# A new late half of a hand-written issue order in a fused S5 scan and Hedgehog attention kernel

## Chip, cores and metric

The kernel runs on one core of one Trainium2 chip. Its time is the device time in microseconds (us) of one execution; where several executions are shown, the median counts. Lower is better. Engines are named as the profile names them: PE (TensorE), PEld (its weight loads), DVE (VectorE), ACT (ScalarE), POOL (GpSimd) and SP (SyncE, which here only issues DMAs).

## What is computed

Two sequence mixers run on the same 2048 x 512 input, and a gate mixes them row by row. Branch `a` is a diagonal complex state space model: a projection, a linear recurrence over 2048 steps, a projection back and a skip term. Branch `b` is linear attention with 32 heads of 16 channels, whose feature map is two softmaxes.

```python
g = sigmoid((x * gate_w).sum(-1, keepdims=True))
# a: state space model
Bu = einsum("bld,pd->blp", x + 0j, B_bar)
for t in range(L):
    h = Lam_bar[None, :] * h + Bu[:, t, :]
a = 2.0 * einsum("blp,dp->bld", hseq, Cmat).real + x * Dskip
# b: linear attention, phi(u) = [softmax(u), softmax(-u)] of 16 channels through w_phi
kv = einsum("bhsf,bhsd->bhfd", phi_k, v)
z = einsum("bhsf->bhf", phi_k)
num = einsum("bhqf,bhfd->bhqd", phi_q, kv)
den = einsum("bhqf,bhf->bhq", phi_q, z)[..., None] + 1e-6
b = reshape(num / den) @ wo
return g * a + (1 - g) * b
```

## The kernel before

The 2048 rows are 16 tiles of 128 rows, regrouped so that a tile holds every eighth row; `order[n]` says which tile is the n-th in the late part. The recurrence is cut into eight residues of the row number: a scan over 256 steps is done for residue 7 (`st_z`), and the other residues follow from it by small diagonal products (`st_h`, PE product `ph`, lines 657 to 676).

The work is written as some 270 small generators, each of which issues a few instructions and yields. One string, `ORDER`, lists their names; the loop at lines 817 to 827 takes a name at a time and lets that generator go on to its next yield. PE, DVE, ACT and SP then keep exactly the order in which the list issued their instructions; each engine runs its own queue in order and waits on semaphores where an operand comes from another engine or from a DMA. So the list is a schedule by hand. A name can carry `@` and digits, the PSUM banks (of eight) that its products take, and `:D` or `:A`. `:D` lets DVE instead of ACT copy or scale a PSUM tile; `:A` lets ACT instead of SP issue an output DMA.

The late half of the list is made of these:

- `q4` to `q15`: queries of tile n, four PE products of 512 columns (line 476), copied into `Xq`.
- `h..`: states of one residue, two or four PE products of 256 columns.
- `X1` to `X3`, `N1` to `N3`, `E1` to `E3`, `S1` to `S3`: the feature map of the queries in groups of four tiles. `X` and `N` are DVE maximum and minimum trees and a subtraction, `E` is four ACT exponentials of 1024 columns (line 534, recorded at line 139), `S` is a DVE sum tree, ACT logarithm and exponential, a DVE product, and four DMA transposes on SP that make `phT` (line 564). Group 3 feeds tiles 12 to 15.
- `y0` to `y15`: branch `a` of tile n in a PSUM bank `py`: eight products of 512 columns (line 718), then four of 128 columns (line 723).
- `o0` to `o15`: branch `b` before the output projection. For each of two halves, four PE products of 68 columns give `pn` (line 737); then ACT takes the logarithm of the denominators (`ld`, line 740) and ACT or DVE copies the numerators (`nu`, line 741). ACT makes `rd` (line 743), DVE multiplies (`on`, line 745), and the result is transposed into `oT`: for n below 12 by a DMA on SP (line 759), for 12 to 15 by four PE transposes into a bank `po` and a copy (lines 751 to 757).
- `t0` to `t15`: four products of 512 columns with `Wo` added to `py` (line 766), the gate scaling to `ot` (lines 775 to 780), and the output DMA (lines 782 to 786). For n = 14 (`LAST`) the scaling and the DMA go in two halves, one on ACT, the other on DVE.

Two resources tie these together. A PSUM bank can be written again only when the engines that read its last contents are done; where ACT's `ld` and DVE's `nu` read the same `pn`, DVE waits for ACT, and PE for DVE. And each DMA has one of eight semaphores (named DMAHW0 to DMAHW7 in the order rows); a DMA waits, on the engine that issues it, until the last DMA on the same semaphore has landed.

Of the kernel before, what the change touches and what calls it, by code (L numbers as in the profile page):

```python
# [36 lines left out]
R6 g23@3 v12@2 c4 c0 c0 g63@5 nA z2 z2 a3 a3 g03@4 xA g03 z2 z2 z2 z2 xA g23 z2 z2 g33@6 c5 v12 z2 z2 g13@0 g13 g63  # L37
g43@4 h32@3 g13 nA g43 h52@2 h52 g33 h32 h61@5 h61 h12@0 c0 g53@4 h12 g33 g53 s4 v14@3 c2 eA eA h42@2 h42 g73@6 g53 eA
eA g73 g73 q10@5 sA h11@0 h11 O h00@4 g73 sA v13@2 h00 v13 a4 z3 sA v15@6 z3 v15 h20@0 h01@4 h30@2 v14 h20 sA h30 z3
h31@6 z3 z3 sA a4 h01 h31 c6 c6 sA q13@3 q13 z3 a4 a4 Y Y h22@0 G q10 z3 z3 G q6@2 q6 h22 z3 z3 sA sA Y Y c1 c1 q9@4  # L40
q8@6 q5@7 h62@3 h41@5 c3 h41 c1 c3 c3 h13@0 h62 q11@2 h13 q11 q8 q12@1 c6 q12 h21@5 q5 h21 h02@2 c7 q4@6 q4 h53@3 h53
h23@1 h23 h33@0 h33 sA q9 h40@7 h40 sA q7@5 h43@6 h63@3 c7 h43 q7 c7 y4@0 y4 sA h63 sA h03@1 END h02 o0@4 o0 X1 N1
o1@7 o1 q14@6 X1 N1 h03 o0@5 X1 o1@2 o1 o1 o0 o0 q15@3 o2@4 o2 o2@7 o2 N1 q15 X1 N1 X1 N1 E1 E1 y2@1 y1@2 y1 E1 E1 q14
X2 y0@5 y0 o1 y4 X2 N2 X2 o0 o0 o3@4 o3 o3@7 o3 o1 o3 y2 X2 N2 o2 X2 N2 S1 S1 N2 S1 o3 S1 N2 S1 S1 o3 y5@3 o2 o2 S1 S1
S1 y1 E2 E2 E2 E2 y9@6 G N3 y5 y5 y3@4 y2 X3 X3 N3 t1 G t1 N3 S1 N3 S2 y9 y9 S2 S2 S1 S1 S2 y3 y3 t3 y0 t0 t0 t2 t2
y6@7 X3 t2:A o4@2 o4 o4@5 o4 o4 y6 y6 t3 X3 o4 X3 o4 S2 S2 t3 o5@1 o5 o5@2 o5 o5 y13@5 y13 o5 N3 o6@4 S2 o6 o6@1 o6 o6
y12@2 o5 y7@4 y7 y12 o6 o6 t4 y7 S2 S2 t4:D S2 E3 E3 E3 E3 S2 o7@1 o7 t5 t5 S3 o7@0 o7 S3 o7 t6 S3 o7 S2 o7 y8@1 o8@3
t6 o8 o8@0 o8 o8 S3 S3 y12 t0:A y11@7 o8 o8 o9@3 o9:D o9@0 o9:D S3 y8 y8 o9 o9 S3 S3 o9 o10@3 y11 o10 o10@0 y11 o10
o10 S3 y14@3 S3 y14 t7 t7:D t8 y14 t8 y15@0 o11@4 S3 o11 o11@1 t9 o12@4 o11:D o11 S3 o10 o10 o12 o12@1 o12 o12 t9:D
o11 y15 o13@4 o13:D o13@6 t6:A o13 o13 o11 o12 y10@1 o14@4 y15 o14:D o12@6 t9 o12:D t7:A t1 y10 y10 o13 o15@4 o15  # L50
o15@6 t4:A t5 o15 o15 t8 o15 t12 t12 t12:A t10 o14@4 o14 o14 t10:D o13@6 t11 o15@2 o15 t10 o13:D t11 t11:A y13 t13 o14
o14@1 t15 t13 t13 t15 t15 o14:D t14 t14 t14:A
"""
H_VECTOR = tuple((r, j) for r in (1, 2, 4, 5, 6) for j in range(4))
OT_PE = (12, 13, 14, 15)
# [805 lines left out]
```

## Time and profile before

| | us |
|---|---|
| median of 3 executions | 157.1 (155.83 to 157.33) |
| profiled execution, its own time | 155.2 |
| span of its instructions | 153.1 |
| PE busy | 147.5 (96%) |
| DVE busy | 133.1 (87%) |
| ACT busy | 129.3 (84%) |
| POOL busy | 15.8 (10%), nothing after the first quarter |

The span runs from the first to the last instruction of the program; the profiled execution's own time has 2.1 us around it. In a view of instructions a row is: start, duration, engine, line, operation, tiles written and read, and in square brackets the idle time of that engine before it with what ended it. `SPq` and `ACTq` are DMA issues. In grouped views the number behind `x` counts instructions and the last ones are busy time and mean duration in ns. "to landing" is the time from the issue of a DMA to its completion.

### The profile page before, as it was taken

How to read it: one execution, taken by the hardware profiler on the slowest of the kernel's cores; microseconds unless marked ns; L12 is line 12 of the kernel's file. 1: busy time of each engine (PE TensorE's matmuls, PEld its weight loads, DVE VectorE, ACT ScalarE, POOL GpSimd, SP SyncE). 2: the span in 40 equal slices, each digit the busy share in tenths (PEclk: the TensorE clock that was granted, in tenths of full speed). 3: DMA queues.
4: the chain of work that ended last, by engine and by line, in shares of the span. 5: the costliest groups of instructions: out<-in, count | busy, mean ns of one | idle time of the engine just before them, and what ended most of it. 6: DMA issues, size and time to landing. Idle time of an engine off the chain costs nothing.

```text
span 153.1 us, 3382 instructions
## 1 busy us (share of the span) xinstructions
PE 147.5 (96%) x1254; PEld 95.5 (62%) x1254; DVE 133.1 (87%) x304; ACT 129.3 (84%) x279; POOL 15.8 (10%) x43
## 2 busy tenths in 40 slices
PE   7999979999999999999999999999999999999990
PEld 7844434788878986869867656555555555546550
DVE  3799999999999999999999999999999858716441
ACT  3589998999998999999998999699488998618471
POOL 8239980000000000000000000000000000000000
PEclk9999999999999999999999999999999999999999
DMA  4785996494455699720000007911159959989943
GB/s 122 158 215 77 232 160 143 99 79 104 103 107 100 133 222 178 167 97 4 0 0 4 0 0 167 76 37 33 36 98 144 178 125 187 168 139 186 255 145 104
DMA packets 50992, 17.55 MB, mean 115 GB/s; under 512 B 44192, under 2 KB 50976, under 8 KB 50976
## 3 DMA queue, kind: packets, MB, share of 16 engines
q1 hardware_dynamic: 49120, 15.82, 57.0%
q10 hardware_dynamic: 1696, 1.51, 3.1%
q8 instruction: 10, 0.16, 0.5%
q0 software_dynamic: 160, 0.01, 0.2%
q14 instruction: 6, 0.05, 0.2%
HBM read 2.64 MB, written 2.10 MB: 31 GB/s over the span
## 4 chain that ended last, share of the span: by engine, by line
PE 80%; SPq 9%; DMA 8%; issue 1%; DVE 0%; ACT 0%
PE pgq L602 18%; PE py L718 16%; PE py L766 9%; PE pq L476 9%; SPq L230 7%; DMA xT<-in_A_x_dram 5%; PE pk L476 5%; PE pv L476 5%; PE ph L669 4%; DMA phT<-EEq 3%; PE kvacc L579 3%; PE pn L737 3%; PE pgq L607 2%; PE py L723 2%; PE pgq L609 2%; SPq L285 1%
## 5 line engine op out<-in xcount | busy, mean ns | idle before, releaser
L602 PE MATMUL pgq<-xT,BT 128*128 128x256 bf16 x256 | 31.5, 273 | 0.0
L476 PEld LDWEIGHTS <-xT 128*128 128x128 bf16 x192 | 18.1, 97 | 19.2 <-DMA xT<-in_A_x_dram 1.7
L602 PEld LDWEIGHTS <-BT 128*128 128x128 bf16 x256 | 24.6, 98 | 4.1
L139 ACT ACTIVATE EEk<-EEk 128x1024 bf16<-128x1024 bf16 x20 | 20.5, 1082 | 0.0
L120 ACT CAST uv<-pgq 128x512 bf16<-128x512 f32 x28 | 15.9, 605 | 0.7 <-PE pgq L602 0.5
L766 PE MATMUL py<-Wo,oT 128*128 128x512 bf16 x64 | 15.9, 380 | 0.0
L476 PE MATMUL pv<-Wv,xT 128*128 128x512 bf16 x64 | 15.8, 379 | 0.0
L476 PE MATMUL pq<-Wq,xT 128*128 128x512 bf16 x64 | 15.6, 379 | 0.0
L476 PE MATMUL pk<-Wk,xT 128*128 128x512 bf16 x64 | 14.8, 380 | 0.8 <-DMA xT<-in_A_x_dram 0.8
L139 ACT ACTIVATE EEq<-EEq 128x1024 bf16<-128x1024 bf16 x12 | 11.7, 1043 | 0.2 <-DVE EEq L528 0.2
L139 ACT ACTIVATE ld<-pn 128x16 f32<-128x16 f32 x32 | 6.1, 191 | 6.1 <-PE pn L737 4.7
L778 ACT ACTIVATE ot<-py,G 128x512 bf16<-128x512 f32 x11 | 7.4, 689 | 4.0 <-PE py L766 3.6
L591 ACT ACTIVATE phT<-X,dgB 128x512 bf16<-128x512 bf16 x16 | 10.7, 725 | 0.0
L120 ACT CAST nu<-pn 128x256 bf16<-128x256 f32 x27 | 9.9, 381 | 0.0
L745 DVE TENSOR_TENSOR on<-nu,rd 128x512 bf16<-128x512 bf16 x16 | 6.7, 421 | 3.5 <-ACT rd L139 1.8
L120 ACT CAST Xq<-pk 128x512 bf16<-128x512 f32 x15 | 8.6, 597 | 1.3 <-PE pk L476 1.3
L120 ACT CAST vx<-pv 128x512 bf16<-128x512 f32 x16 | 9.1, 603 | 0.4 <-PE pv L476 0.4
L549 DVE TENSOR_TENSOR EEk<-EEk,rck 128x4096 bf16<-128x4096 bf16 (+1 forms) x5 | 9.3, 1859 | 0.0
L120 ACT CAST Xq<-pq 128x512 bf16<-128x512 f32 x16 | 8.9, 609 | 0.2 <-PE pq L476 0.2
L766 PEld LDWEIGHTS <-oT 128*128 128x128 bf16 x64 | 5.5, 97 | 5.7 <-DMA oT<-on 0.8
L737 PEld LDWEIGHTS <-phT 128*128 128x128 bf16 x128 | 6.3, 97 | 3.5 <-DMA phT<-EEq 0.8
L512 DVE TENSOR_TENSOR smk<-smk 128x512 bf16<-128x512 bf16 (+4 forms) x18 | 8.1, 447 | 0.1
(180 smaller groups left out, 323.9 us busy)
## 6 DMA issues: line engine op xcount, KB each, us to landing
X<-HM SPq DMA_DIRECT2D x8, 256.0 KB, 4.4
out_dram<-ot SPq DMA_DIRECT2D x8, 128.0 KB, 2.2
out_dram<-ot ACTq DMA_DIRECT2D x7, 128.0 KB, 2.7
C2r<-in_B_wqkv_dram ACTq DMA_DIRECT2D x2, 256.0 KB, 3.5
Wv<-in_B_wqkv_dram SPq DMA_DIRECT2D x1, 512.0 KB, 4.1
Bn<-in_A_B_re_dram SPq DMA_DIRECT2D x1, 512.0 KB, 6.4
Bn<-in_A_B_im_dram SPq DMA_DIRECT2D x1, 512.0 KB, 7.2
Wo<-in_B_wo_dram SPq DMA_DIRECT2D x1, 512.0 KB, 4.1
```

What stands on the lines that cost most here:

```text
L120: nc.scalar.copy(out=out_ap, in_=in_ap)
L139: ins = nc.scalar.activation(**kw)
L230: nc.sync.dma_start_transpose(out=xT[:, :, ti * P:(ti + 1) * P], in_=x_res[ti // 2, ti % 2])
L476: MM(out=pt[:], lhsT=xT[:, kt, ti * P:(ti + 1) * P], rhs=W[:, kt, :], start=(kt == 0), stop=(kt == KT - 1))
L512: VT(out=dst, in0=cur[:, :, :, 0:n, :], in1=cur[:, :, :, n:2 * n, :], op=op)
L549: VT(out=E5, in0=E5, in1=rc.to_broadcast([P, L, 2 * NB, Dh, 4]), op=ALU.mult)
L591: nc.scalar.mul(out=t_, in_=x_, mul=c_)
L602: MM(out=pg[:, h, :], lhsT=BT[:, kt, 2 * j + h, :], rhs=xT[:, kt, r * NC:(r + 1) * NC], start=(h == 0 and kt == 0), stop=(r % 2 == 0 and k ...
L718: MM(out=py[:], lhsT=hs(r, t, slice(a * P, (a + 1) * P)), rhs=C2B[t], start=(t == 0), stop=False)
L737: MM(out=pn[:, 4 * m:4 * m + 4, :].rearrange("p h e -> p (h e)"), lhsT=ph[:, 4 * hf + m, :], rhs=KVm[:, 4 * hf + m, :], start=(m == 0), st ...
L766: MM(out=py[:], lhsT=oT[:, g, :], rhs=Wo[:, g, :], start=False, stop=(g == HG - 1))
L778: nc.scalar.mul(out=ot[:], in_=py[:], mul=G[:, ti:ti + 1])
```

## The change

Only the string `ORDER` changes, from the middle of line 40 on: of its 855 names the first 499 stay, and the other 356 are put in another order. The same generators run the same number of times. Other things that the names carry change with it: most PSUM banks, and `:D` or `:A` on some steps, so that three numerator copies and three gate scalings that ACT did are now done by DVE. Two lines of the diff, from the end of the list:

```diff
-o15@6 t4:A t5 o15 o15 t8 o15 t12 t12 t12:A t10 o14@4 o14 o14 t10:D o13@6 t11 o15@2 o15 t10 o13:D t11 t11:A y13 t13 o14
-o14@1 t15 t13 t13 t15 t15 o14:D t14 t14 t14:A
+o11 o13@6 o11 t0:A t7:A o12:D o13 t10 y13@4 t10:D t4:A o14@6 o12 t3 t1 t2:A o14:D o13@3 o14@7 y13 o14 o13:D o12 o15@3
+o15:D t11:A t14 t15 t14 t12:A t13 t14:A t15:D t15 t13 t9 t13
```

What it makes of the queues is shown at two places. The first is ACT near the end. The rows are in issue order, the brackets name the semaphores that a row waits for, and the numbers in the tile names tell buffers apart. Before, with `ot_2278` and `ot_2112` the scaled outputs of tiles 7 and 4, and `pn_2415` and `pn_2422` the two products of one tile:

```order
L139 ACTIVATE ld_2351<-pn_2360 128x16 [waits PE_49]
L120 CAST nu_2350<-pn_2360 128x256 [waits DVE_49]
L139 ACTIVATE rd_2352<-ld_2351,nge_85 128x128 [waits Activation_49]
L139 ACTIVATE ld_2379<-pn_2381 128x16 [waits PE_49]
L786 DMA out_0_dram<-ot_2278 128x512 [waits DMAHW5_49]
L139 ACTIVATE ld_2413<-pn_2415 128x16 [waits PE_49]
L120 CAST nu_2412<-pn_2415 128x256 [waits DVE_49]
L786 DMA out_0_dram<-ot_2112 128x512 [waits DMAHW0_49]
L139 ACTIVATE ld_2413<-pn_2422 128x16 [waits PE_49]
L120 CAST nu_2412<-pn_2422 128x256
```

Now, with `ot_2140` and `ot_2026` the outputs of tiles 4 and 2, `pn_2384` and `pn_2400` the products of tile 14, and `pn_2395` the second product of tile 13:

```order
L786 DMA out_0_dram<-ot_2140 128x512 [waits DMAHW4_49]
L139 ACTIVATE rd_2323<-ld_2322,nge_85 128x128 [waits Activation_49]
L786 DMA out_0_dram<-ot_2026 128x512 [waits DMAHW6_49]
L139 ACTIVATE ld_2382<-pn_2384 128x16 [waits PE_49]
L139 ACTIVATE ld_2382<-pn_2400 128x16 [waits PE_49]
L120 CAST nu_2381<-pn_2400 128x256 [waits DVE_49]
L139 ACTIVATE ld_2353<-pn_2395 128x16
L139 ACTIVATE rd_2354<-ld_2353,nge_85 128x128 [waits Activation_49]
```

Before, the last output that waits for a transpose of `oT` (DMAHW0) stands between the logarithms of the two halves of one tile. Now such an output (DMAHW6) stands ahead of three logarithms, of `pn_2384`, `pn_2400` and `pn_2395`.

The second place is SP's queue over the same stretch, from the last transposes of tiles below 10 on. Before:

```order
L759 DMA_TRANSPOSE oT_2233<-on_2200 128x4x128 [waits DMAHW3_49,DVE_49,PE_49]
L564 DMA_TRANSPOSE phT_2262<-EEq_2018 128x8x128 [waits DMAHW4_49,DVE_49,PE_49]
L564 DMA_TRANSPOSE phT_2262<-EEq_2018 128x8x128 [waits DMAHW5_49,Activation_49]
L564 DMA_TRANSPOSE phT_2262<-EEq_2018 128x8x128 [waits DMAHW6_49,Activation_49]
L564 DMA_TRANSPOSE phT_2262<-EEq_2018 128x8x128 [waits DMAHW7_49,Activation_49]
L759 DMA_TRANSPOSE oT_2330<-on_2235 128x4x128 [waits DMAHW0_49,DVE_49]
L759 DMA_TRANSPOSE oT_2369<-on_2295 128x4x128 [waits DMAHW1_49,DVE_49]
```

Now:

```order
L759 DMA_TRANSPOSE oT_2296<-on_2201 128x4x128 [waits DMAHW1_49,DVE_49,PE_49]
L564 DMA_TRANSPOSE phT_2318<-EEq_2089 128x8x128 [waits DMAHW2_49,DVE_49,PE_49]
L564 DMA_TRANSPOSE phT_2318<-EEq_2089 128x8x128 [waits DMAHW3_49,Activation_49]
L564 DMA_TRANSPOSE phT_2318<-EEq_2089 128x8x128 [waits DMAHW4_49,Activation_49]
L564 DMA_TRANSPOSE phT_2318<-EEq_2089 128x8x128 [waits DMAHW5_49,Activation_49]
L759 DMA_TRANSPOSE oT_2360<-on_2281 128x4x128 [waits DMAHW6_49,DVE_49]
L786 DMA out_0_dram<-ot_1985 128x512 [waits DMAHW0_49]
```

The four `phT` transposes of group 3 are followed by one `oT` instead of two. That one, `oT_2360` of tile 11, is the last user of DMAHW6 before ACT's output `ot_2026`. In both lists the first `oT` behind group 3 is the 77th DMA of SP's queue. From the 62nd to the 76th stood fourteen transposes and one output; now there are fifteen transposes and no output.

Behind these DVE reads, in the new list, the products of tiles 14 and 13, and PE writes the first product of tile 15 into the bank of the second product of tile 13:

```order
L122 CAST nu_2321<-pn_2345 128x256 [waits Activation_49]
L780 TENSOR_SCALAR ot_2377<-py_2238,G_84 128x512 [waits PE_49]
L122 CAST nu_2381<-pn_2384 128x256 [waits DVE_49,Activation_49]
L122 CAST nu_2352<-pn_2395 128x256 [waits PE_49,Activation_49]
L745 TENSOR_TENSOR on_2320<-nu_2321,rd_2323 128x512 [waits DMAHW0_49,DVE_49]
L745 TENSOR_TENSOR on_2380<-nu_2381,rd_2383 128x512 [waits DMAHW1_49,DVE_49,Activation_49]
L745 TENSOR_TENSOR on_2351<-nu_2352,rd_2354 128x512 [waits DMAHW6_49,DVE_49]
```

DVE's copies of `pn_2384` and `pn_2395` stand ahead of the three multiplications for tiles 12, 14 and 13. On PE, between the three products of tiles 14 and 13 and the first product of tile 15 (`o15@3`), stand four products of 512 columns, the second half of `y13`.

More of the change, by code (lines that the diff above doesn't have):

```diff
@@ L39 @@
 eA g73 g73 q10@5 sA h11@0 h11 O h00@4 g73 sA v13@2 h00 v13 a4 z3 sA v15@6 z3 v15 h20@0 h01@4 h30@2 v14 h20 sA h30 z3
[L40 to L48, printed above, removed]
@@ L49 @@
-o10 S3 y14@3 S3 y14 t7 t7:D t8 y14 t8 y15@0 o11@4 S3 o11 o11@1 t9 o12@4 o11:D o11 S3 o10 o10 o12 o12@1 o12 o12 t9:D
-o11 y15 o13@4 o13:D o13@6 t6:A o13 o13 o11 o12 y10@1 o14@4 y15 o14:D o12@6 t9 o12:D t7:A t1 y10 y10 o13 o15@4 o15
-o15@6 t4:A t5 o15 o15 t8 o15 t12 t12 t12:A t10 o14@4 o14 o14 t10:D o13@6 t11 o15@2 o15 t10 o13:D t11 t11:A y13 t13 o14
-o14@1 t15 t13 t13 t15 t15 o14:D t14 t14 t14:A
+h31@6 z3 z3 sA a4 h01 h31 c6 c6 sA q13@3 q13 z3 a4 a4 Y Y h22@0 G q10 z3 z3 G q6@2 q6 Y z3 sA h21@7 z3 q4@6 q11@5 q4
@@ new lines @@
+h62@2 c1 h40@3 h21 h22 q9@6 c3 h13@0 q14@7 h40 h53@3 h33@4 q9 q8@6 h62 c1 c3 h41@2 sA Y c1 q7@1 h33 q11 h43@5 c3 sA c7
+h13 c7 h53 h43 q7 c6 q14 q5@0 h63@3 h23@5 sA h03@1 h02@7 q8 h41 h23 q5 c7 h63 h03 sA sA y0@6 END X1 o1@0 h02 N1 q15@1
+y2@7 X1 o0@3 y4@5 N1 X1 o0 N1 o2@3 X1 o0@2 o1 o1@0 N1 q15 X1 N1 o0 o2 o0 o1 o1 X2 y2 o1 E1 G y3@1 o3@0 X2 N2 y1@4
+q12@3 X2 o0 X2 E1 N2 o2@2 X2 E1 E1 y0 o2 y3 S1 o0 N2 y4 o3 y1 o3@0 S1 N2 S1 o3 o3 q12 y8@2 o1 y5@0 y8 y2 o3 o2 S1 y6@3
+o3 S1 N2 S1 S1 E2 y3 o2 y0 t0 E2 S1 N3 N3 y5 G y1 E2 t3 X3 o2 t1 X3 N3 X3 E2 t2 t0 S2 t1 y9@6 S1 y5 S2 S2 o4@4 t3 S1
@@ new lines @@
+o4 y8 S2 S1 o4@1 y6 o4:D S2 o4 y4 N3 S2 S2 y11@1 S1 X3 t2 o5@4 o5 o5@7 o4 o5 y11 o6@4 o6 o6@7 o4 y9 S2 y9 o6 o7@7 X3
+o5 o6 o7 y7@4 y6 S2 N3 o7@7 t4 S2 y11 E3 o5 o7:D E3 o8@7 o6 y7 t4:D o8 o9@7 y14@5 o7 o7 S2 o6 o5 E3 y7 o9:D E3 o9@7
+y14 o9:D o7 o8@7 o9 S3 o8 t6 o10@7 t5 o9 o8 o8 S2 y14 t6 o8 o10 t5 S3 S3 S3 o10@3 y10@7 o10:D y12@0 y12 S3 o9 S3 y10
+o10 t7 y10 t8 y12 o11@3 S3 o10 o11 S3 o10 t8:D t9 o11@3 y15@2 t7:D o11 S3 o12@3 S3 S3 t9:D o11 y15 o12 S3 y15 o12@3
+o11 o13@6 o11 t0:A t7:A o12:D o13 t10 y13@4 t10:D t4:A o14@6 o12 t3 t1 t2:A o14:D o13@3 o14@7 y13 o14 o13:D o12 o15@3
@@ L53 @@
+y13 t8 t5 o13 o14 o15 t10 o12@7 o15@6 o14 o13 t11 o15:D o12 o13@3 o14@7 t12 o15 t6:A o15 o15@6 o14:D o13 t11:D t12
+o15:D t11:A t14 t15 t14 t12:A t13 t14:A t15:D t15 t13 t9 t13
 """
```

## Prediction

> **What bounds the kernel now.** I read the busy time by stretch first (columns: stretch and its length, then busy us and instruction count of PE, PEld, DVE, ACT and POOL, granted PE clock, DMA share, GB/s).
>
> ```profile
> 90.00:100.00 10.00, 10.00 (x75) 6.22 (x74) 9.96 (x21) 8.41 (x19) 0.00 (x0) 1.00 0.68 93
> 120.00:130.00 10.00, 9.90 (x73) 4.93 (x71) 7.79 (x12) 9.35 (x28) 0.00 (x0) 1.00 0.82 158
> 130.00:140.00 10.00, 9.98 (x82) 5.27 (x81) 5.16 (x11) 5.19 (x22) 0.00 (x0) 1.00 0.98 160
> 140.00:150.00 10.00, 9.52 (x85) 5.27 (x83) 4.49 (x11) 6.55 (x20) 0.00 (x0) 1.00 0.70 191
> 150.00:153.10 3.10, 0.00 (x0) 0.00 (x0) 0.48 (x1) 0.03 (x1) 0.00 (x0) 0.88 0.33 106
> ```
>
> PE is busy all the time at a granted clock of 1.00; DVE and ACT have room from 120 us on, and the DMA engines do not. The changed half of the list begins at about 87 us, before the first of these rows. No PE instruction is taken out, so the change can win only PE's waits and the 3.6 us behind its last product. Whether a busy PE runs at its rate is read from the chain of waits (start, length, what):
>
> ```profile
> 133.07 1.73 PE py L718 x8
> 141.41 0.22 PE py L723 x4
> 130.39 0.25 PE pn L737 x8
> 147.79 1.74 PE py L766 x8
> ```
>
> A product of 512 columns takes 1.73/8 = 0.216 us, one of 128 columns 0.055, one of 68 columns 0.032; the last ends at 147.79 + 1.74 = 149.53. The timeline around the largest wait:
>
> ```profile
> 120.11 1.03 PE L718 MATMUL py<-C2i,Bn 128*128 128x512 bf16 x4
> 121.23 0.31 PEld L737 LDWEIGHTS <-phT 128*128 128x128 bf16 x8 [0.59 <-DMA phT<-EEq]
> 121.24 0.43 PE L737 MATMUL pn<-KVm,phT 128*128 128x68 bf16 x8
> ```
>
> Four products from 120.11 need 0.86 us, the next starts at 121.24: 0.27 us lost to a transpose that landed late, though the drawn end (1.03 us, 0.16 too long) hides part of it. In the three stretches to 149.53 the visible idle time is 0.10 + 0.02 + 0.01; where it shows, 0.16 more is hidden. That makes some 0.45 us, and a few waits under 0.16 that cannot be seen. I take 0.6 us for all PE waits in the changed half, 0.3 at least.
>
> **What the change can give.** The 0.6 us, if every late transpose goes. How the transposes come late is seen in the DMA view of 97 to 100 us, and in the view of the `phT` and `oT` tiles (issue duration min/median/max in ns; time to landing), the two `oT` answers from 105 to 112.5 us and from 139.9 us on:
>
> ```profile
> q8 instruction: 1, 0.02, 3.8%
> phT<-EEk SPq DMA_TRANSPOSE x1, 4.9
> DMA to landing us min/median/max: 2.7/3.3/4.9
> L564 SPq DMA_TRANSPOSE phT<-EEq x12: 1247/1292/2247, 113.1 to 138.7; - x12
> DMA to landing us min/median/max: 2.4/2.4/2.5
> DMA to landing us min/median/max: 3.0/3.4/3.8
> ```
>
> A transpose in flight beside an instruction load (queue q8) landed after 4.9 us, others of its kind after 2.7. So a load costs the transfers, not PE directly. [...]
>
> DVE's dependent instructions: the timeline has the same engine with and without a dependence.
>
> ```profile
> 113.68 0.69 DVE L512 TENSOR_TENSOR mxq<-Xq 128x1024 bf16<-128x1024 bf16 x1
> 114.40 0.43 DVE L512 TENSOR_TENSOR mxq<-mxq 128x512 bf16<-128x512 bf16 x1
> 114.74 0.42 DVE L512 TENSOR_TENSOR mnq<-mnq 128x512 bf16<-128x512 bf16 x1
> ```
>
> The second needs the first and starts 0.72 us behind it, 0.03 after its end; the third needs neither, and starts 0.34 behind, 0.09 before the end. A dependence on the row just above costs 0.12 us. The late list has nine waits of a DVE row for the row just above before and eight after, so DVE gains about 0.1 us, and PE, which does not wait for DVE where these stand, nothing.
>
> The three copies and three scalings that go from ACT to DVE, by these groups of the late part,
>
> ```profile
> L122 DVE CAST nu<-pn 128x256 bf16<-128x256 f32 x5 | 2.0, 423 | 2.7 <-ACT ld L139 2.7
> L780 DVE TENSOR_SCALAR ot<-py,G 128x512 bf16<-128x512 f32 x4 | 3.0, 748 | 4.1 <-PE py L766 4.1
> L778 ACT ACTIVATE ot<-py,G 128x512 bf16<-128x512 f32 x11 | 7.4, 689 | 4.0 <-PE py L766 3.6 <-ACT ot L778 0.4
> L139 ACT ACTIVATE EEq<-EEq 128x1024 bf16<-128x1024 bf16 x12 | 11.7, 1043 | 0.2 <-DVE EEq L528 0.2
> ```
>
> cost DVE 3 x (0.42 + 0.75) = 3.5 us where it is idle for 2.2 + 4.8 + 5.5 us from 120 on. That cover hides them: 0, unless one stands ahead of a copy that PE waits for, then up to 0.75. The moved queries, states and trees between 87 and 120 us I also cost at 0 (PE has no idle time there before), 0.5 if a state comes late.
>
> **What it costs: a wait on ACT that PE does not cover.** In the new list ACT issues the output of tile 2 on DMAHW6, the semaphore of `oT_2360`, and behind it come the logarithms of tile 14 and of tile 13's second half. Such a wait is in the trace of before (timeline from 140 us):
>
> ```profile
> 140.09 2.54 SPq L759 DMA_TRANSPOSE oT<-on  x2
> 140.34 0.34 ACTq L786 DMA_DIRECT2D out_dram<-ot  x1
> 140.72 0.18 ACT L139 ACTIVATE ld<-pn 128x16 f32<-128x16 f32 x1 [0.21 <-issue]
> 140.80 0.37 ACT L120 CAST nu<-pn 128x256 bf16<-128x256 f32 x1
> 143.04 1.91 PE L766 MATMUL py<-Wo,oT 128*128 128x512 bf16 x8
> 143.88 0.34 ACTq L786 DMA_DIRECT2D out_dram<-ot  x1
> 143.96 0.43 DVE L745 TENSOR_TENSOR on<-nu,rd 128x512 bf16<-128x512 bf16 x1 [1.54 <-DMA oT<-on]
> 144.28 0.18 ACT L139 ACTIVATE ld<-pn 128x16 f32<-128x16 f32 x1 [0.72 <-PE py L766]
> ```
>
> The first `oT` behind group 3 was issued at 140.09; at 143.88 ACT issues the output that waits for it, and at 143.96 DVE goes on that waits for the same. Landing: 143.88, 3.8 us after the issue, the worst of that view. Only one logarithm stood behind it, and PE had 1.9 us of `t` products just then. Now the same in the new list, step by step.
>
> When PE is due at the first product of tile 15: behind it, up to the end, stand 20 products of 512 columns, 20 of 128 and 8 of 68: 4.32 + 1.10 + 0.26 = 5.7 us. From 149.53 less 0.6 (the waits gone) plus 0.4 (below), that is 149.33 - 5.7 = 143.6.
>
> When `oT_2360` lands: in before, the thirteen transposes ahead of 140.09 began at
>
> ```profile
> 122.06 1.20 SPq L759 DMA_TRANSPOSE oT<-on  x1
> 121.61 0.35 SPq L786 DMA_DIRECT2D out_dram<-ot  x1
> 119.74 1.36 SPq L759 DMA_TRANSPOSE oT<-on  x1
> ```
>
> so they took (140.09 - 122.06)/13 = 1.39 us each, without a pause. In the new list fourteen follow straight on the transpose that stood at 119.74, and could begin at 121.1, at 121.5 if that one waits as long for DVE as now plus 0.4. 121.3 + 14 x 1.39 = 140.8; at least 140.1, if none meets an instruction load. With 3.0 to 3.8 us to landing, or 2.4 on a quiet queue, it lands at 142.5 to 144.8. I take 144.1, by the middle 3.4, since three outputs are issued beside it.
>
> From landing to PE: issue to next logarithm 0.38 (140.34 to 140.72), two logarithms and a copy on ACT 0.08 + 0.08 + 0.26, the logarithm of tile 13 0.18, DVE's copy 0.42, and 0.1 for three hand-overs: 1.5 us, 1.3 to 1.7. So PE goes on at 145.6 instead of 143.6: it waits 1.9 us (0.2 with 142.5 and 1.3; 2.9 with 144.8 and 1.7).
>
> Second, tiles 7 to 9 send five products through bank 7 between 125 and 131 us, with group 3's exponentials between the logarithms on ACT. A round is PE 0.3, up to 0.9 behind an exponential of 1.04, logarithm 0.18, DVE copy 0.42, hand-overs 0.1: 1.9 at worst, 1.0 at best. PE has 0.13 of product, then 0.86 + 0.22 for half a `y`: 1.2. Wait 0 to 0.7; I take 0.4.
>
> Third, the end. Before and after the last product:
>
> ```profile
> 150.06 0.48 DVE L773 TENSOR_SCALAR ot<-py,G 128x256 bf16<-128x256 f32 x1 [1.81 <-ACT ot L772]
> 150.57 0.33 SPq L784 DMA_DIRECT2D out_dram<-ot  x1
> out_dram<-ot SPq DMA_DIRECT2D x8, 128.0 KB, 2.2
> out_dram<-ot SPq DMA_DIRECT2D x1, 64.0 KB, 1.6
> ```
>
> The last tile is now 13, scaled whole: 0.69 us instead of the 1.04 to 150.57, but 128 KB that land in 2.2 us instead of 1.6, behind two more outputs on SP (0.1): +0.35, between 0 and +0.6.
>
> **Sum:** -0.6 + 1.9 + 0.4 + 0.35 = +2.05 us. The profiled span would be 155.15, its execution 157.25; from the median, 157.1 + 2.05 = **159.1**, 1.3% slower. With the ends of the large wait and the medians of the rest: 157.4 to 160.1; the forecast's own range is 158.2 to 160.2, with the small terms.
>
> **Rivals.** *The wait is covered.* The transposes run at the 2.4 us of the quiet rows, ACT passes almost unheld, PE loses 0.2: -0.6 + 0.2 + 0.4 + 0.35 = +0.35, 157.4, no change. It decides from a landing of `oT_2360` at about 142.5 or earlier. For it: four rows at 2.4 to 2.5. Against: those stood in a queue with pauses; where it was full, 3.0 to 3.8.
>
> *Transfers come in time everywhere.* The timed runs have 1.9 us more than the profiled one (157.1 to 155.2); if that is late transposes that instruction loads pushed, and the new places spare them, and all three new waits stay away, -0.6 to -1.9: 155.2 to 156.5. Against it, the queue of transposes is longer than before by one.
>
> *A load falls into group 3's transposes.* PE's loads come every 250 or so instructions; one near 133 us has the last `oT` and `phT` issues behind it. Its 2.2 us, less the 0.9 or so that PE has in hand for `phT`, come on top: +1.3, 160.4.
>
> **How the numbers follow.** Forecast 0.58, covered wait 0.22, all in time 0.08, load in group 3 0.12. The range 156.9 to 160.6 leaves out the second rival and half of the third, some of the forecast's own ends: 0.18. One per cent, about what a measurement of this kernel tells from no change, is 1.57 us: slower means above 158.67, which is four fifths of the forecast (0.47) and the third rival (0.12), 0.59; faster, below 155.53, half of the second (0.04) and a little, 0.05; the rest 0.36.
>
> **What would show it.** Right: PE idle for 1 to 3 us near 145 in front of `pn` L737, ended by DVE `nu`, DVE waiting for ACT `ld`, and ACT's `ld` right behind an `ACTq` output that starts when `oT` lands; a small gap near 128; no wait for `phT`. Wrong: PE passing 145 without idle time, an `oT` landing within 2.5 us there, or PE waiting for `ph` or `KVm` between 87 and 115, which I cost at nothing.

## The result and the profile after

| | before | after |
|---|---|---|
| median of 4 executions, us | 156.47 (155.06 to 157.33) | 160.49 (158.83 to 162.52) |
| ratio | | 1.0267, 95% interval 1.0212 to 1.0322 |
| profiled execution, us | 155.2 | 161.47 |
| its span | 153.1 | 159.3 |

The changed kernel is 2.7% slower; the forecast was 1.3%. The ratio leaves out the executions that were counted as slow, here two of the changed kernel (161.47 and 162.52); by the medians of all it is 160.49/156.47 = 1.026. The changed kernel's executions fall into two groups by their mean granted clock: in this measurement and its repetition four had 0.979 to 0.988 and took 160.9 to 162.5 us, four had 0.996 to 0.998 and took 158.8 to 159.5. The profiled one is of the first group: behind PE's longest wait its granted clock was 0.50 for 3.41 us, from 148.59 to 152.01. Executions of that group are said below to have the half clock.

The busy time by stretch, of the changed kernel (columns as in the prediction):

```profile
120.00:130.00 10.00, 9.67 (x91) 5.42 (x90) 7.50 (x12) 8.93 (x28) 0.00 (x0) 1.00 0.72 137
130.00:140.00 10.00, 9.40 (x67) 4.69 (x64) 7.22 (x14) 4.33 (x15) 0.00 (x0) 1.00 0.80 115
140.00:150.00 10.00, 6.73 (x63) 3.77 (x64) 3.51 (x8) 4.05 (x17) 0.00 (x0) 0.93 0.81 202
150.00:159.30 9.30, 5.57 (x30) 2.80 (x28) 3.08 (x6) 2.52 (x5) 0.00 (x0) 0.87 0.30 100
```

Most of the loss is between 140 and 150 us: PE is busy for 6.73 instead of 9.52 us, and the granted clock is 0.93 instead of 1.00. The timeline of the changed kernel shows what PE waited for:

```profile
127.06 0.30 PE L737 MATMUL pn<-KVm,phT 128*128 128x68 bf16 x4 [0.33 <-DMA phT<-EEq]
136.99 5.44 SPq L564 DMA_TRANSPOSE phT<-EEq  x4
140.28 0.30 PE L737 MATMUL pn<-KVm,phT 128*128 128x68 bf16 x4 [0.88 <-DMA phT<-EEq]
142.52 1.90 SPq L759 DMA_TRANSPOSE oT<-on  x1
144.02 0.56 PE L737 MATMUL pn<-KVm,phT 128*128 128x68 bf16 x12 [0.36 <-DMA phT<-EEq]
146.52 0.38 ACTq L786 DMA_DIRECT2D out_dram<-ot  x1
146.94 0.26 ACT L139 ACTIVATE ld<-pn 128x16 f32<-128x16 f32 x2 [2.16 <-DMA oT<-on]
147.16 0.85 DVE L122 CAST nu<-pn 128x256 bf16<-128x256 f32 x2 [3.57 <-ACT ld L139]
148.07 0.29 PE L737 MATMUL pn<-KVm,phT 128*128 128x68 bf16 x4 [2.62 <-DMA out_dram<-ot]
148.91 1.90 PE L766 MATMUL py<-Wo,oT 128*128 128x512 bf16 x4
150.60 1.06 PE L754 MATMUL po<-ident,on 128*128 128x128 bf16 x8
```

`oT_2360` is issued at 142.52 and lands where ACT can issue the output that waits for it, at 146.52. Behind that come ACT's logarithms (146.94), DVE's copies (147.16) and the first product of tile 15 (148.07). The releaser named in PE's bracket is the output issued at 146.52; what PE needs is the bank that DVE's copies free. The four products of 512 columns that start at 148.91 then take 1.69 us up to the next one (150.60; the drawn end of 1.90 is too long), 0.42 each instead of 0.216, at a granted clock of 0.50. Three waits for `phT` stand ahead of it.

From the starts of successive products, where the forecast's method takes 0.216, 0.055 and 0.032 us for each, PE waits 0.50 + 1.04 + 0.52 + 2.79 = 4.85 us from 126 on. At a clock of 0.50 for 3.41 us it loses up to 1.7. With 0.12 more up to 79 us, 0.6 less for the waits of before, and an end of 3.76 instead of 3.62 us behind the last product, that is 0.12 + 4.85 + 1.7 - 0.6 + 0.14 = 6.2 us, the difference of the spans (159.3 - 153.1). The 1.7 is an upper bound and the 0.6 the prediction's estimate, so the agreement to the tenth is partly luck.

### The profile page after: what moved, and what is told of

It reads as the page before. It is cut to its first block, busy times and chain, and to the rows that moved or that the text cites. A ratio compares the mean times of both kernels' runs of the same rounds, so it can differ in the third digit from the quotient of the medians.

```text
span 159.3 us, 3391 instructions
## 1 busy us (share of the span) xinstructions
PE 149.2 (94%) x1254; PEld 96.2 (60%) x1254; DVE 136.2 (85%) x310; ACT 127.5 (80%) x273; POOL 15.2 (10%) x43
## 4 chain that ended last, share of the span: by engine, by line
PE 75%; DMA 10%; SPq 10%; ACT 1%; issue 1%; DVE 0%
PE pgq L602 18%; PE py L718 14%; PE pq L476 9%; PE py L766 8%; SPq L230 6%; DMA xT<-in_A_x_dram 5%; PE pk L476 5%; PE pv L476 4%; DMA phT<-EEq 4%; PE ph L669 4%; PE kvacc L579 3%; PE pn L737 2%; PE pgq L607 2%; PE py L723 2%; PE pgq L609 2%; SPq L285 1%
## 5 line engine op out<-in xcount | busy, mean ns | idle before, releaser
L766 PE MATMUL py<-Wo,oT 128*128 128x512 bf16 x64 | 16.9, 399 | 0.0
L476 PE MATMUL pq<-Wq,xT 128*128 128x512 bf16 x64 | 16.1, 379 | 0.0
L737 PE MATMUL pn<-KVm,phT 128*128 128x68 bf16 x128 | 8.4, 196 | 4.2 <-DMA out_dram<-ot 2.6
L737 PEld LDWEIGHTS <-phT 128*128 128x128 bf16 x128 | 6.9, 99 | 8.7 <-DMA phT<-EEq 3.3
L122 DVE CAST nu<-pn 128x256 bf16<-128x256 f32 x9 | 3.8, 424 | 8.8 <-ACT ld L139 8.8
L766 PEld LDWEIGHTS <-oT 128*128 128x128 bf16 x64 | 6.0, 103 | 5.4 <-issue 0.8
L120 ACT CAST nu<-pn 128x256 bf16<-128x256 f32 x23 | 8.5, 383 | 0.0
```

Source lines behind the costliest of these rows:

```text
L120: nc.scalar.copy(out=out_ap, in_=in_ap)
L476: MM(out=pt[:], lhsT=xT[:, kt, ti * P:(ti + 1) * P], rhs=W[:, kt, :], start=(kt == 0), stop=(kt == KT - 1))
L737: MM(out=pn[:, 4 * m:4 * m + 4, :].rearrange("p h e -> p (h e)"), lhsT=ph[:, 4 * hf + m, :], rhs=KVm[:, 4 * hf + m, :], start=(m == 0), st ...
L766: MM(out=py[:], lhsT=oT[:, g, :], rhs=Wo[:, g, :], start=False, stop=(g == HG - 1))
```

## Experiments

Each kernel was timed beside the kernel before, whose median was 155.6 us for the first three told here and for the one made from before, 155.5 for the four that follow on those three, 155.2 for the two with a halved end and the one with six products in the wait, and 155.4 for the last. Differences in us between kernels are those of medians; the ratios, which come from fewer runs, give smaller ones in places, and both are said where that matters. The diffs show only the changed stretch of a line of the list; `...` stands for lines left out.

**The changed kernel again**, as the measure for the rest.

> The changed kernel once more, timed and profiled beside its variants. Theory A (the place of ACT's output): PE idle 1.5 to 3 us in front of the first product of tile 15, ended by DVE's copy of tile 13's second half, which waits for ACT, which waits for the transpose of tile 11. Theory B (SP's queue): PE idle 0.3 to 1.1 us each in front of three products that wait for phT, two of them of group 3. [...] Time 1.5% to 4% above the kernel before.

160.16 us (158.85 to 160.96), ratio 1.0255 [1.0184, 1.0326]. The waits are there again: 0.45 near 127, 0.84 at 139, and 3.19 in front of tile 15, without the one at 143 and with a longer one behind it.

**Outputs of tiles 4 and 2 behind the logarithms of tile 15.** Only ACT's order changes; the transposes on SP stay.

```diff
-t10:D t4:A o14@6 o12 t3 t1 t2:A o14:D
+t10:D o14@6 o12 t3 t1 o14:D
...
-o13 o14 o15 t10
+o13 o14 o15 t4:A t2:A t10
```

> ACT's outputs of tiles 4 and 2 stand behind the first logarithm of tile 15 instead of ahead of those of tiles 14 and 13; nothing else is moved. Theory A: the wait of 2.8 us in front of the first product of tile 15 falls to 0.7 or less, what is left waits for the transpose of tile 11 itself, and no product runs at half rate; the waits for phT stay at 0.3 to 1.1 us each. Time 1.0% to 1.8% above the kernel before. Theory B alone (SP's queue sets everything): the wait stays near 2.8 us under another name, since PE needs the same transposes, and the time stays 2% to 4% above.

158.07 us (157.45 to 158.18), ratio 1.0141 [1.0102, 1.0180]. In its timeline, and in the view of its four last `phT` transposes, behind the rows of the largest wait:

```profile
146.12 0.30 PE L737 MATMUL pn<-KVm,phT 128*128 128x68 bf16 x4 [1.01 <-DMA phT<-EEq]
146.46 0.34 ACTq L786 DMA_DIRECT2D out_dram<-ot  x1
...
DMA to landing us min/median/max: 3.3/3.3/4.8
```

The wait for ACT is gone, and with it the half clock in all four executions (clock 0.996 or more). In its place stands a wait for the fourth `phT`, which landed 4.8 us after its issue: 1.01 us, more than the 0.7 that was expected to be left. So the order on ACT is worth 160.16 - 158.07 = 2.1 us (1.8 by the ratios), half clock included; 2.2 to 2.5 us of loss have another cause.

**Two transposes fewer.** The `oT` transposes of tiles 8 and 10 are not made; their `t` products read the transpose of the tile before.

```diff
-        nc.sync.dma_start_transpose(out=oT[:], in_=on2.rearrange("p g f -> p (g f)"))
+        if n in (8, 10):
+            live["oT", n] = live["oT", n - 1]
+        else:
+            nc.sync.dma_start_transpose(out=oT[:], in_=on2.rearrange("p g f -> p (g f)"))
```

> The transposes of tiles 8 and 10 are not made; these two tiles' output products read the transposed tile before (so two output tiles differ from the reference's). SP's queue ahead of group 3's phT is two entries, 2.6 us, shorter; ACT's output still waits for the transpose of tile 11. Theory B: the two waits for group 3's phT (1.0 and 0.5 us) vanish, the one for group 2 (0.5) stays, and the wait in front of tile 15 shrinks from 2.8 to 0.3 to 1.2 us. Time 0.3% to 1.2% above the kernel before. If the late phT came from their sources (DVE's product, ACT's exponentials) and not from the queue, the 1.0 and 0.5 us stay.

159.64 us (159.07 to 160.26), ratio 1.0251 [1.0206, 1.0296]: 0.5 us less by the medians, 0.06 by the ratios, too little to be told from nothing, and against the expectation. Its timeline:

```profile
135.16 5.38 SPq L564 DMA_TRANSPOSE phT<-EEq  x4
140.63 1.79 SPq L762 DMA_TRANSPOSE oT<-on  x1
145.28 0.34 ACTq L789 DMA_DIRECT2D out_dram<-ot  x1
146.79 0.29 PE L737 MATMUL pn<-KVm,phT 128*128 128x68 bf16 x4 [2.81 <-DVE nu L122]
```

Group 3 came 1.8 us earlier and PE's waits for it are gone, so PE came earlier to tile 15 too. But `oT_2360`'s counterpart landed 4.65 us after its issue, so that the wait there stayed at 2.8 us, and PE went on at 146.79, only 1.3 us earlier than in the changed kernel's profile. And all four executions had the half clock (0.986 to 0.989), where half of the changed kernel's had it. Against those of the changed kernel with the half clock (median 161.2 us) the 159.64 are 1.6 us less. So the transposes were worth something here too, and a wait that ends later, with the half clock behind it, hid most of it in the medians; why all four had the half clock, no run shows.

**Both edits at once** show what the transposes are worth without that wait.

> The changed kernel with both edits of before at once: the outputs of tiles 4 and 2 behind the logarithms of tile 15's first half, and the transposes of tiles 8 and 10 not made (their output is that of another tile's transpose). If the loss that is left after the outputs are moved is SP's queue of transposes (its group 3 comes some 2 us later than PE needs it), group 3's transposes start at 135.0 to 135.3 instead of 137, PE's waits between 139 and 146 (0.78 and 1.17 in the kernel with the outputs moved) are gone, and the time is 156.2, ratio 0.998 to 1.008. If the queue is only one of several waits that end together (PE comes earlier and then waits for DVE or ACT instead), over half of the 1.95 us stays, and the ratio is over 1.010.

155.99 us (155.81 to 156.45), ratio 1.0033 [1.0002, 1.0064]. Busy time by stretch and timeline:

```profile
130.00:140.00 10.00, 9.89 (x72) 5.27 (x73) 7.11 (x14) 4.67 (x16) 0.00 (x0) 1.00 0.88 129
140.00:150.00 10.00, 9.69 (x85) 5.29 (x83) 6.40 (x14) 5.32 (x18) 0.00 (x0) 1.00 0.72 201
...
134.90 5.38 SPq L564 DMA_TRANSPOSE phT<-EEq  x4
```

PE is busy for 9.69 us of the last stretch. With the outputs out of the way the two transposes are worth 158.07 - 155.99 = 2.1 us (1.7 by the ratios); with the outputs in the way the medians showed 0.5, or 1.6 between executions with the half clock.

**Tile 10 transposed by PE**, with the outputs moved back and nothing left out: the same relief by one transpose, in a kernel that computes everything.

```diff
-OT_PE = (12, 13, 14, 15)
+OT_PE = (10, 12, 13, 14, 15)
...
-S3 o10 t8:D t9 o11@3 y15@2 t7:D o11 S3 o12@3 S3 S3 t9:D
+S3 t8:D t9 o11@3 y15@2 t7:D o11 S3 o12@3 o10@4 S3 S3 t9:D o10:D
```

> The changed kernel with the outputs of tiles 4 and 2 moved back, and tile 10 transposed by PE (four transposes of 128 columns through bank 4, copied by DVE) instead of by a DMA on SP; nothing is left out of the computation. One transpose fewer in SP's queue: group 3's start 1.3 us earlier, at 135.5 to 136; PE does 4 x 0.055 = 0.22 us more. By the theory of the queue the waits 0.78 and 1.17 shrink to 0.6 together, so 158.07 + 0.22 - 1.3 = 157.0, ratio 1.003 to 1.011. By the rival (other waits end at the same time) 158.0 to 158.5, ratio 1.013 or more.

156.64 us (155.95 to 156.93), ratio 1.0054 [1.0020, 1.0088]: 1.4 us for one transpose, the four PE products paid. The theory of the queue holds.

**Instruction loads 3.4 us earlier.**

```diff
-NR F:28 NI B
+NR F:56 NI B
...
-                MM(out=spin[:, 0:P], lhsT=fillw[:], rhs=fillw[:], start=True, stop=True)
+                w = P // 2 if eng == "56" else P
+                MM(out=spin[:, 0:w], lhsT=fillw[:], rhs=fillw[:, 0:w], start=True, stop=True)
```

> The changed kernel with 56 fill products of 64 columns at its very start instead of 28 of 128: 28 products and their weight loads more, so every later instruction load of PE comes some 56 instructions, about 3.4 us, earlier; the late list is as it is. The load at 131 to 131.6, beside which an issue took 2.4 us instead of 1.3 and a transpose landed after 4.5 us instead of 3.3, moves to about 128, the one at 117.5 to about 114, the one at 150.5 to about 147. If the load at 131 is what makes group 3 late, group 3's transposes start up to 1 us earlier, the first wait (0.84 at 139) goes, and the time is 159.0 to 159.5, ratio 1.018 to 1.022. If the place of the load is worth nothing, since it delays the queue by as much wherever it falls in it, the time is 159.8 to 160.6, ratio 1.023 to 1.030.

164.57 us (163.66 to 165.01), ratio 1.0554 [1.0470, 1.0637]. Neither expectation: 4.4 us worse than the changed kernel. All four executions had the half clock (0.979 to 0.986); against those of the changed kernel that had it (161.2) it is 3.4 us. The DMA view from 146 to 150 us, the view of the `oT` transpose of tile 11, and the timeline:

```profile
q8 instruction: 1, 0.02, 1.5%
...
DMA to landing us min/median/max: 5.6/5.6/5.6
...
143.33 2.06 SPq L759 DMA_TRANSPOSE oT<-on  x1
148.94 0.34 ACTq L786 DMA_DIRECT2D out_dram<-ot  x1
150.45 0.39 PE L737 MATMUL pn<-KVm,phT 128*128 128x68 bf16 x4 [4.54 <-DVE nu L122]
```

One load stands in the view from 146 to 150 us, where the changed kernel has none (its last is at 150.95); the transpose of tile 11, in flight from 143.33 on, took 5.6 us instead of 4.0, and PE waited 4.5 us. Two other transposes, near 98 and 130 us, came late as well (PE waits of 0.80 and 0.89). So an edit that moved the loads cost several us. What part of it is that load and what the outputs and the queue beside it, this run doesn't tell; five outputs on SP, issued from 145.44 on, were in flight beside the same transpose.

**The outputs of tiles 0 and 7 moved behind as well** (beside those of 4 and 2).

```diff
-o11 t0:A t7:A o12:D
+o11 o12:D
...
-t11 o15:D
+t11 o15:D t0:A t7:A
```

> The changed kernel with the outputs of tiles 4 and 2 moved back, and besides them the two outputs of tiles 0 and 7, which ACT issues at 140.2 and 140.8 beside the last transposes, moved behind the logarithms of tile 15. If 256 KB of outputs beside the transposes is what makes the last phT (4.1 to 5.0 us from issue to landing) and the oT behind it (4.0 to 4.6) slow, these fall to 3.5 or less, the wait at 144.7 falls from 1.17 to 0.5 or less, and the time is 157.3, ratio 1.006 to 1.012. If the transposes are as slow among themselves, nothing changes: 157.8 to 158.4, ratio 1.012 to 1.018.

157.75 us (157.18 to 158.03), ratio 1.0111 [1.0026, 1.0197]. The last four `phT` and the `oT` behind them, and the timeline:

```profile
DMA to landing us min/median/max: 3.3/3.3/3.3
...
DMA to landing us min/median/max: 2.4/2.4/2.4
...
146.49 0.94 ACTq L786 DMA_DIRECT2D out_dram<-ot  x2
147.47 0.58 ACT L120 COPY oT<-po 128x512 bf16<-128x512 bf16 x1 [0.82 <-issue]
148.10 0.38 PE L754 MATMUL po<-ident,on 128*128 128x128 bf16 x4 [0.95 <-ACT oT L120]
```

The transposes are as fast as on a quiet queue: 3.3 instead of up to 4.8 us, 2.4 instead of 3.7. Yet only 0.3 us came of it by the medians, and the executions overlap with those of the run with two outputs moved (157.45 to 158.18): the two outputs now stand on ACT ahead of the copy that PE waits for, 0.95 us.

**The mechanism in the kernel before.** The outputs of tiles 7 and 4 on ACT (and that of tile 1 on SP between them) are put ahead of the logarithms of tiles 14 and 12; that of tile 4 then waits for a `phT` of group 3.

```diff
-y15 o14:D o12@6 t9 o12:D t7:A t1
+y15 t7:A t1 t4:A o14:D o12@6 t9 o12:D
...
-o15@6 t4:A t5
+o15@6 t5
```

> The kernel before with ACT's outputs of tiles 7 and 4 ahead of the first logarithm of tile 14 instead of behind it and in tile 15; the later of them waits for the last phT of group 3, which landed at 142.35 in the profile shown, while ACT reached that logarithm at 141.44. Theory A: the logarithm starts at about 142.7, 1.3 us later, and PE waits 0.4 to 1.0 us for the bank that tile 15's first product takes; time +0.3% to +0.6% to the kernel before. Theory B alone: no transposes move, so no new PE wait, time within 0.2%.

156.63 us (155.76 to 157.41, 10 executions), ratio 1.0057 [1.0022, 1.0092]. The chain is that of the changed kernel:

```profile
143.80 0.34 ACTq L786 DMA_DIRECT2D out_dram<-ot  x1
144.19 0.18 ACT L139 ACTIVATE ld<-pn 128x16 f32<-128x16 f32 x1 [2.03 <-DMA phT<-EEq]
144.88 0.62 PE L737 MATMUL pn<-KVm,phT 128*128 128x68 bf16 x8 [1.18 <-DVE nu L122]
```

An output in a wrong place on ACT costs PE 1.2 us here, a little more than the 0.4 to 1.0 expected, and no half clock follows.

**A halved end, and two outputs on SP.** From the kernel with tile 10 on PE: first tile 13 scaled in two halves, then besides the outputs of tiles 0 and 7 issued by SP behind the last transpose.

```diff
-LAST = 14
+LAST = 13
...
-o11 t0:A t7:A o12:D
+o11 t0 t7 o12:D
```

> The kernel with the outputs of tiles 4 and 2 moved back and tile 10 transposed by PE, and tile 13, the last of all, scaled in two halves (ACT and DVE, 64 KB each) in place of tile 14. If a whole last tile of 128 KB is what the end costs more than before (forecast 0.35 us, 0 to 0.6), the stretch behind PE's last product falls from 3.9 to 3.5 us and the time is 156.2, ratio 1.002 to 1.004. If the end is set by something else (the queue of outputs on SP and ACT), it stays at 156.4 to 156.8, ratio 1.005 to 1.008.

> The kernel with the halved end, and besides the two outputs of tiles 0 and 7 issued by SP behind the last transpose instead of by ACT beside the last transposes. With the outputs behind, the last phT should land after 3.3 us and the oT after 2.45 (4.2 and 3.5 with ACT's outputs beside them); ACT is spared two issues of 0.39 us, and unlike in the run with four outputs behind on ACT no copy of ACT waits for them. Forecast 0.2 to 0.5 us less than the kernel with the halved end alone: 155.8, ratio 0.999 to 1.003. By the rival (PE's waits there end by DVE, not by a transpose) no difference, ratio 1.002 to 1.005.

156.10 us (155.60 to 156.41), ratio 1.0055 [1.0036, 1.0073], and 155.88 us (155.54 to 156.25), ratio 1.0045 [1.0027, 1.0063]. Halving the end gave nothing that can be told: the median is 0.5 us lower, but so was that of the kernel before beside it by 0.3, and the ratio is the same (1.0055 and 1.0054). In its timeline

```profile
150.60 0.47 ACT L772 ACTIVATE ot<-py,G 128x256 bf16<-128x256 f32 x1 [1.04 <-PE py L766]
151.11 0.48 DVE L773 TENSOR_SCALAR ot<-py,G 128x256 bf16<-128x256 f32 x1 [0.62 <-ACT ot L772]
151.62 0.33 SPq L784 DMA_DIRECT2D out_dram<-ot  x1
```

the halves follow each other, and the issue at 151.62 comes 1.05 us after the last product, against 0.89 with a whole tile; the shorter transfer (1.76 instead of 2.05 us) pays that and 0.1 more. The outputs on SP made the transposes fast (3.3 and 2.5 us) without the new wait on ACT; the time fell by 0.2 us, within what the two intervals leave open. No version here beats the kernel before.

**Products in the long wait.** The changed kernel with six, then twelve products of a zero matrix, added to tile 13's branch `a` right ahead of the first product of tile 15. They change no result and no other order.

```diff
-y13 o14 o13:D o12 o15@3
+y13 o14 o13:D o12 Z:6 o15@3
...
+        if tok == "Z":
+            for _ in range(int(eng)):
+                MM(out=live["py", 13][:], lhsT=zerow[:], rhs=Wo[:, 0, :], start=False, stop=False)
+            continue
```

> The changed kernel with six products of 512 columns of a zero matrix added to tile 13's branch a (they add 0) right ahead of the first product of tile 15, in the long wait: 6 x 0.216 = 1.3 us of it is filled, and nothing else is moved. If the half clock after the wait comes from PE standing idle for about 3 us, PE is idle for 1.5 to 1.9 us only, the granted clock stays 1.0 up to the last product, the 1.1 to 1.3 us lost to half rate come back, and the time is 158.9 to 159.2, ratio 1.016 to 1.020. If the half clock has another cause, it stays, and the time is that of the changed kernel, 160.0 to 160.4, ratio 1.024 to 1.028.

> The changed kernel with twelve instead of six zero products in the long wait: 12 x 0.216 = 2.6 us of it is filled. [...] Median 159.2, ratio 1.020 to 1.028. By the rival, that the half clock comes from the load on the chip or from chance, about half of the executions have it, with a clock of 0.979 to 0.989 and 160.8 us or more.

Six: 159.55 us (158.49 to 161.61), ratio 1.0248 [1.0215, 1.0280]. Two of six executions still had the half clock (161.3 and 161.6 us, 0.986 and 0.988), the others took 158.5 to 159.9. Twelve: 159.47 us (159.40 to 160.21), ratio 1.0281 [1.0244, 1.0319], and none of six had it (0.995 to 1.000). Busy time in stretches of 3.41 us, in the first two kernels around the point where the granted clock falls, first of the changed kernel (the repetition), then with six, then with twelve products:

```profile
144.69:148.10 3.41, 0.51 (x11) 0.60 (x12) 1.41 (x4) 1.49 (x8) 0.00 (x0) 1.00 0.94 280
148.10:151.51 3.41, 3.19 (x22) 2.03 (x20) 1.62 (x5) 1.80 (x5) 0.00 (x0) 0.50 0.14 43
```

```profile
145.55:148.96 3.41, 1.36 (x18) 0.84 (x17) 1.52 (x5) 1.60 (x8) 0.00 (x0) 1.00 0.90 260
148.96:152.37 3.41, 3.41 (x21) 1.90 (x18) 1.71 (x6) 1.69 (x5) 0.00 (x0) 0.50 0.13 42
```

```profile
143.50:146.92 3.42, 3.37 (x21) 1.57 (x19) 0.02 (x1) 0.29 (x4) 0.00 (x0) 1.00 1.13 254
146.92:150.33 3.41, 2.73 (x32) 1.82 (x31) 2.95 (x8) 3.01 (x11) 0.00 (x0) 1.00 0.43 145
150.33:153.74 3.41, 3.32 (x19) 1.41 (x17) 2.33 (x5) 1.26 (x4) 0.00 (x0) 1.00 0.31 99
```

A stretch with 0.51 or 1.36 us of PE is followed by one at a clock of 0.50, one with 2.73 by one at 1.00; in the first profile of the changed kernel PE was busy for 0.79 us of the 3.41 us ahead of the 0.50. If the half clock came in half of all executions whatever PE did, six in a row without it would be one case in 64. The counts are few, and the runs were made on other chips than the repetition; they make PE's own wait the likely cause, and how long a wait it takes was not shown. The time is not 159.2 but 159.5, about what the executions of the changed kernel without the half clock took (158.8 to 159.5).

## Why the prediction was right or wrong

**The wait on ACT: right mechanism, wrong size.** Every link is there, in order: the output held until `oT` lands, logarithms, copies, PE. From landing to PE it took 1.57 us (146.50 to 148.07) where 1.5 was forecast. But `oT_2360` was issued at 142.52, not 140.8 nor within 140.1 to 141.0, and landed 3.98 us later, not 3.4. PE waited 2.79 (3.19 in the repetition) instead of 1.9, though it came to tile 15 at 145.3 (148.07 less the 2.79) and not at 143.6. The forecast's own figures, 144.1 + 1.5 - 143.6, give 2.0 where it wrote 1.9. Moving the two outputs shows the term's worth: 2.1 us with the half clock.

**"No wait for phT" is the step that failed.** The sum gave group 3's transposes no term, on the argument that the last late transposes go and that PE has 0.9 us in hand. The queue of SP had one transpose more and no pause, began 0.74 us later than taken (122.04 for 121.3), and met an instruction load; its fourteen transposes took 20.48 us, 1.46 each instead of 1.39. In the view of the `oT` transposes from 130 to 143 us, and the DMA view from 129 to 133, of the changed kernel:

```profile
L759 SPq DMA_TRANSPOSE oT<-on x5: 1207/1222/2414, 129.2 to 142.5; - x5
...
q8 instruction: 1, 0.02, 2.6%
```

one issue took 2.41 us instead of 1.22, ahead of group 3, which is what the third rival described with a load near 133 us (+1.3). The kernel before met a load there as well: the view of its `oT` transposes from 130 to 134.5 us has

```profile
L759 SPq DMA_TRANSPOSE oT<-on x3: 1199/1225/1705, 130.2 to 132.8; - x3
```

and a load at 133.1, so that the forecast's 1.39 us already held 0.5 us for one load; the new list paid 1.2. The run with both edits has an issue of 2.41 us too, at 131.4, and still ended within 0.5 us of the kernel before, so this issue alone does not make the loss. So the forecast, kept apart from that rival, and the rival happened together: late `phT` of group 3 cost 1.04 + 0.52 at 139 and 143 us, and the same delay pushed `oT_2360`. Why the queue began 0.74 us late was not pursued. The runs give 2.1 us for two transposes of the queue once the outputs are out of the way.

**The half clock was in no term.** A wait of 1.9 us was priced at 1.9 us. In half of the executions the half clock follows: their median is 161.2 us against 159.15, 2.05 more, of which the 3.41 us at 0.50, measured in the profile, explain 1.7; the rest was not pursued.

**The small terms.** The bank round of tiles 7 to 9 was priced at 0.4: PE waited 0.50 near 127, but for a `phT` of group 2, and in the repetition 0.27 for that and 0.18 in front of a later product, where the run with both edits shows one of 0.16 for DVE's copy. So the size came out mostly by another cause, which is luck. The end was priced at 0.35 and measured at 0.14; halving the last tile changed the end by 0.1 at most. The 0.6 us of before's waits did go (the one at 121 us fell from 0.27 to 0.07), and the work between 87 and 115 us cost nothing, as forecast.

Put together from the runs, with the edits taken in this order, of the 4.6 us between the medians 155.58 and 160.16, 2.1 are the outputs on ACT (about 1.0 of it half clock), 2.1 the queue of transposes ahead of group 3, and 0.4 what is left with both edits (155.99).

On the loads, where a transpose is in flight: beside a load an `oT` issue took 1.71 us in the kernel before and 2.41 in the changed one, against medians of 1.23 and 1.22 in the same views. The run with the loads moved, 164.57 for 160.16 us, has a transpose at 5.6 us and a load in the view beside it, but does not tell the load from the outputs.

## What to carry to other kernels

In this program an output DMA on ACT's queue waited for the transfer that last used its semaphore (`oT_2360`, landed 3.98 us after its issue), and ACT stood idle for 2.16 us ahead of the next logarithm; what stands behind such an output should be work that nobody needs soon. Where two late inputs end near each other, removing one can show little until the other is gone (the two transposes: 0.5 us by the medians, then 2.1), so an edit with little effect should be tried again together with the next one. When a new order leaves a DMA queue without pauses, each step it feeds gets a landing time worked out and set against the time its reader is due, the load that the queue will meet included (here an issue of 2.41 us instead of 1.22).

## What the runs showed of the hardware

In the profile of the changed kernel the granted clock was 1.00 up to 148.59 us, 0.50 from there to 152.01, and 1.00 again while PE's last products ran. In the 3.41 us ahead of the 0.50 PE was busy for 0.79 us; in the repetition it was 0.51, with six zero products 1.36. After stretches of the same length with 2.73 us (twelve zero products) and 2.41 us (two outputs moved, 142.95 to 146.37) the clock stayed at 1.00. What lies between 1.36 and 2.41 these rows don't show, nor why the same kernel has both times: no profile shows the changed kernel without the half clock.

With two outputs of 128 KB issued beside the last transposes a `phT` landed after 4.8 us and the `oT` behind it after 3.7; with these outputs moved behind, it was 3.3 and 2.4. In the run with two outputs on SP it was 3.3 and 2.5.
